# The forward 47-point stage of a Fourier mixing kernel, in four 64x64 quarters of TensorE's array

## The chip, the cores and the metric

One core of a Trainium2 chip runs the whole program. The metric is the device time of one execution in microseconds (us); the time before is the median of three runs.

## The reference

```python
X = np.fft.rfft(x, axis=1)                    # x: 8 batches, 3008 rows, 256 channels
y = np.fft.irfft(X * (filt_r + 1j * filt_i), n=3008, axis=1)
h = y.reshape(24064, 256) @ w_in              # 256 x 2048
s = np.sin(alpha * h)
return (h + s * s / (alpha + 1e-09)) @ w_out  # 2048 x 256
```

A filter is applied along the sequence in the frequency domain, and a two-layer network with a sine follows on each row.

## The kernel before, in words

**The transform.** 3008 is 47 x 64. A row of x is 64 m + r with m from 0 to 46 and r from 0 to 63, the residue. The forward transform is done in two stages: 47-point transforms over m for each residue (the stage that changes), then 64-point transforms over the residues for each of 24 kept frequencies. The spectrum is multiplied by the filter, and two inverse stages lead back. Data is fp16, sums are fp32.

**Batch 0** is kept on the chip (f1_chip, turn1, g_chip, turn2) and is not touched. **Batches 1 to 7** go by these steps, each a small function:

- load_x (L130 to L138) brings x to the tile xt by GpSimd's DMA queue, which turns fp32 into fp16. A partition holds one m and one of two residue groups (a = 0 for residues 0 to 31, a = 1 for 32 to 63), 94 partitions; along the partition lie the 32 residues of the group, 256 channels each. Each part of a load is two transfers (80 and 14 partitions). Batch 1 comes in four parts, the others in two.
- f1 (L140 to L152) is the 47-point stage. Its table wa is block-diagonal: 94 rows (two groups of 47) by 96 columns (two groups of 24 real and 24 imaginary parts), with zeros between the groups. Unit u, of 16, multiplies it with residues 2u and 2u + 1 of both groups (512 moving elements, L145) into one PSUM bank, psa. ScalarE copies even units to the tile asb, VectorE odd ones (L146). After units 7 and 15, SyncE stores half of asb to scratch memory (L150).
- shuffle1 (L197 to L202) reads the scratch back in another order as bint, in three transfers on SyncE's queue (the gather).
- f2x (L204 to L211) is the 64-point stage, product (L213 to L229) the filter, f2g (L231) the first inverse stage, with a scratch store and shuffle2 (L246) as gather; f3 (L252) is the second inverse stage, which writes yt, the network's input.

**The network.** For each chunk g of 512 rows (47 chunks) mlp_in (L276) makes 16 blocks of 128 hidden units: two matmuls of 512 moving elements into a bank ph (L281) and a sine on ScalarE (L283). VectorE squares them (L288), and the previous chunk's second layer goes by mlp_out (L300) or, for some chunks, by fast_out (L380), which uses seven block products instead of eight with sums on VectorE (L331, L391).

**What sets the order.** The program order is written by hand. The loop over g has eight slots a chunk; each slot has two mlp_in calls with parts of the previous chunk's second layer between them. A plan gives for each half slot the steps of the transform that are put there, so that batch b's transform runs inside the network of batch b - 1. For batches 2 to 7 two f1 units stand in the first half of each of eight slots; for batch 1 one unit stands in each of sixteen half slots, from slot 4 on. shuffle1 is put eight slots after the first unit, the first f2x at slot x0, and load_x of the next batch near the last product. Each engine works its instructions in order; each DMA queue does so too. GpSimd's queue carries the loads of x, the filter and the weights, in this order for batch 1: w_in (L602), x of batch 1, w_out (L452). SyncE's queue carries the scratch stores, the gathers and the output. PSUM banks for f1, f2x, f2g, f3 and parts of the set-up come from one pool, psf, of three. xt and bint share one buffer, so a batch's x is loaded once bint of the batch before is read.

At the start there is one small matmul for alpha (psal, L446: a 16-row fp32 operand), followed by matmuls on zeros that keep TensorE busy (keep_busy, L496).

Of the kernel before, what the change touches and what calls it, by code (L numbers as in the profile page):

```python
# [9 lines left out]
FP16 = mybir.dt.float16  # L10
FP32 = mybir.dt.float32
# [3 lines left out]
B, S, C, DFF = 8, 3008, 256, 2048  # L15
MT, R, NK, RP = 47, 64, 24, 32
GT = 2 * MT


def dft_tables():  # L20

    m = np.arange(MT)
    k1 = np.arange(NK)
    ang = 2 * np.pi * np.outer(m, k1) / MT
    fa = np.concatenate([np.cos(ang), -np.sin(ang)], 1) / np.sqrt(MT)
    wa = np.zeros((MT, 2, 2, 2 * NK))
    wa[:, 0, 0] = fa  # L30
    wa[:, 1, 1] = fa
    wa = wa.reshape(2 * MT, 4 * NK)
    wa2 = wa.reshape(2 * MT, 4, NK).transpose(0, 2, 1).reshape(2 * MT, 4 * NK)

    we = wa.T.copy()
    we2 = wa2.T.copy()
    r = np.arange(R)
    wb = np.zeros((2, R, NK, 128))
    wg = np.zeros((128, NK, 2, R))
    q = 1 / np.sqrt(R)  # L40
    d, j, di, ji = slice(0, 32), slice(32, 64), slice(64, 96), slice(96, 128)
    for s in range(NK):
        kd = s + MT * np.arange(32)
        kj = MT * np.arange(1, 33) - s
        td = 2 * np.pi * (np.outer(r, kd) % S) / S
        tj = 2 * np.pi * (np.outer(r, kj) % S) / S
        cd, sd, cj, sj = np.cos(td) * q, np.sin(td) * q, np.cos(tj) * q, np.sin(tj) * q
        wb[0, :, s, d], wb[1, :, s, d], wb[0, :, s, di], wb[1, :, s, di] = (
            cd, sd, -sd, cd)
        wb[0, :, s, j], wb[1, :, s, j], wb[0, :, s, ji], wb[1, :, s, ji] = (  # L50
            cj, -sj, -sj, -cj)
        wd = np.where((kd == 0) | (kd == S // 2), 1.0, 2.0)[:, None]
        wj = np.where(kj == S // 2, 1.0, 0.0 if s == 0 else 2.0)[:, None]
        wg[d, s, 0], wg[di, s, 0], wg[d, s, 1], wg[di, s, 1] = (
            wd * v.T for v in (cd, -sd, sd, cd))
        wg[j, s, 0], wg[ji, s, 0], wg[j, s, 1], wg[ji, s, 1] = (
            wj * v.T for v in (cj, -sj, -sj, -cj))

    wb = wb.reshape(2, 2, RP, NK * 128).transpose(2, 1, 0, 3).reshape(128, NK * 128)
    wg = wg.reshape(128, NK, 2, 2, RP).transpose(0, 1, 4, 3, 2).reshape(128, NK * 128)  # L60
    wgs = np.concatenate([wg[64:], -wg[:64]], 0)
    return [a.astype(np.float16) for a in (wa, wb, wg, we, wa2, we2, wgs)]

@with_exitstack
def kernel(
# [10 lines left out]
    nc = tc.nc  # L76
# [3 lines left out]
    def dram(ap, off, dims):  # L80
        return bass.AP(tensor=ap.tensor, offset=ap.offset + off, ap=dims)

    wa_np, wb_np, wg_np, we_np, wa2_np, we2_np, wgs_np = dft_tables()
    wa_d = nc.inline_tensor(wa_np, name="wa_tbl")
    wb_d = nc.inline_tensor(wb_np, name="wb_tbl")
    wg_d = nc.inline_tensor(wg_np, name="wg_tbl")
    we_d = nc.inline_tensor(we_np, name="we_tbl")
# [6 lines left out]
    cpool = ctx.enter_context(tc.tile_pool(name="consts", bufs=1))  # L94
    xbpool = ctx.enter_context(tc.tile_pool(name="xbp", bufs=1))
# [3 lines left out]
    agpool = ctx.enter_context(tc.tile_pool(name="agp", bufs=1))  # L99
    ginpool = ctx.enter_context(tc.tile_pool(name="ginp", bufs=2))  # L100
    ypool = ctx.enter_context(tc.tile_pool(name="yp", bufs=4))
    vpool = ctx.enter_context(tc.tile_pool(name="vp", bufs=2))
# [3 lines left out]
    psf = ctx.enter_context(tc.tile_pool(name="psf", bufs=3, space=PSUM))  # L106
    psh = ctx.enter_context(tc.tile_pool(name="psh", bufs=3, space=PSUM))
    pso = ctx.enter_context(tc.tile_pool(name="pso", bufs=1, space=PSUM))

    wa = cpool.tile([GT, 4 * NK], FP16, name="wa")  # L110
    we = cpool.tile([4 * NK, GT], FP16, name="we")
    wa2 = cpool.tile([GT, 4 * NK], FP16, name="wa2")
    we2 = cpool.tile([4 * NK, GT], FP16, name="we2")
    wb = cpool.tile([128, NK * 128], FP16, name="wb")
    wg = cpool.tile([128, NK * 128], FP16, name="wg")
# [6 lines left out]
    xt, asb, scr1, bint, xs, z, t2, gsb, scr2, gin, yt, vt, po, ot, x_dma, w_in_dma, filter_dma = (  # L122
        {} for _ in range(17))
# [5 lines left out]

    def load_x(b, parts=2):  # L130

        xt[b] = (xbpool if b else vpool).tile([GT, RP, C], FP16, name="xt", tag="xb" if b else "vt")
        n = RP // parts
        for h in range(parts):
            for p0, p1 in ((0, 80), (80, GT)):
                x_dma[b, h] = nc.gpsimd.dma_start(  # L136
                    out=xt[b][p0:p1, n * h:n * h + n, :],
                    in_=dram(x, (b * S + RP * p0 + n * h) * C, [[RP * C, p1 - p0], [1, n * C]]))  # L138

    def f1(b, u):  # L140
        if u == 0:
            asb[b] = agpool.tile([4 * NK, RP, C], FP16, name="asb", tag="ag")
            scr1[b] = dpool.tile([RP, 4 * NK, C], FP16, name="scr1", tag="scr1")
        ps = psf.tile([4 * NK, 2, C], FP32, name="psa", tag="f")
        nc.tensor.matmul(out=ps, lhsT=wa, rhs=xt[b][:, 2 * u:2 * u + 2, :], start=True, stop=True)  # L145
        (nc.vector.tensor_copy if u % 2 else nc.scalar.copy)(  # L146
            out=asb[b][:, 2 * u:2 * u + 2, :], in_=ps)
        if u % 8 == 7:
            k = 2 * u - 14
            nc.sync.dma_start(out=scr1[b][k:k + 16].rearrange("r q c -> q r c"),  # L150
                              in_=asb[b][:, k:k + 16, :])

    def f1_chip(k):

# [364 lines left out]
    def at(slot, f, *args):  # L519
        plan.setdefault(int(2 * slot), []).append((f, args))  # L520

    for b in range(1, B):
        p = MT * (b - 1)
        u0, x0, step = (4, 16, 1.1) if b == 1 else (p - 9, p + 4, 1.9)
        for u in range(16):
            at(u0 + u / 2 if b == 1 else u0 + u // 2, f1, b, u)
        at(u0 + 8, shuffle1, b)
        for k in range(6):
            xa, xb = x0 + int(2 * k * step), x0 + int((2 * k + 1) * step)
            at(xa, f2x, b, 2 * k)  # L530
            at(xb, f2x, b, 2 * k + 1)
            at(xb + 1, product, b, k, 0)
            at(xb + 2, product, b, k, 1)
            at(xb + 4, f2g, b, 2 * k)
            at(xb + 5, f2g, b, 2 * k + 1)
        at(xb + 6, shuffle2, b)
        if b + 1 < B:
            at(xb + 1, load_x, b + 1)
# [37 lines left out]
    with tc.manual_schedule():  # L576
# [2 lines left out]
        nc.scalar.dma_start(out=alpha_r, in_=moe_alpha.rearrange("(a p) -> a p", p=128))  # L579
        nc.scalar.dma_start(out=ident32, in_=id32_d.ap())  # L580
        nc.scalar.dma_start(out=we2, in_=we2_d.ap())
        nc.scalar.dma_start(out=wa, in_=wa_d.ap())
        nc.scalar.dma_start(out=we, in_=we_d.ap())
        nc.sync.dma_start(out=wb[:, 0:8 * 128], in_=wb_d.ap()[:, 0:8 * 128])
        zero = spool.tile([128, 512], FP16, name="zero", tag="z")
# [2 lines left out]
        nc.vector.memset(warm, 0.0)  # L588
        nc.scalar.activation(out=warm, in_=warm, func=AFT.Sin)
        load_x(0, 4)  # L590
        wgs = ginpool.tile([128, NK * 128], FP16, name="wgs", tag="gin")
        for s0 in (0, 8, 16):
# [6 lines left out]
        for h in range(2):  # L599
            hs = slice(1024 * h, 1024 * h + 1024)  # L600
            for cb in range(2):
                w_in_dma[h, cb] = nc.gpsimd.dma_start(out=w_in16[:, cb, hs],  # L602
                                                      in_=moe_w_in[128 * cb:128 * cb + 128, hs])
# [21 lines left out]
        for j in range(4):  # L625
            turn2(j)
        load_x(1, 4)
        load_w_out(0)
        load_w_out(1)
# [59 lines left out]
```

## Time and profile before

| what | value |
|---|---|
| median of 3 runs | 822.12 us (821.15 to 822.87) |
| the profiled execution | 823.99 us |
| its span, first to last instruction | 822.1 us |
| granted TensorE clock | 1.000 |
| L145 psa matmuls, 94x96 by 512 | 112, 381 ns each as recorded (median) |
| L145 weights loads of wa | 112, 124 ns |
| L146 copies to asb on ScalarE, VectorE | 56 of 584 ns, 56 of 682 ns |
| L136 loads of x on GpSimd's queue | 40 issues, 544 ns |
| L150 stores of asb on SyncE's queue | 14 issues, 324 ns |
| L201 gathers of bint on SyncE's queue | 21 issues, 424 ns |

A matmul's record is longer than the time for which it keeps the next one from starting, since matmuls are pipelined: how much of TensorE one takes is read from the start of one to the start of the next. PEld is the queue of weights loads, which runs beside the matmuls. Times in text are us from the span's start, if nothing else is said.

### The profile page before, as it was taken

What the parts mean: (1) busy time and instruction counts of PE and PEld (TensorE: products, weight loads), DVE (VectorE), ACT (ScalarE), POOL (GpSimd) and SP (SyncE); (2) the same over time, 40 slices, a digit from 0 to 9 for tenths busy, and PEclk for the clock granted to TensorE, in tenths of its full rate; (3) what the DMA queues carried; (4) which work ended last, traced back from release to release, by engine and by line L of the source; (5) the groups of instructions that cost most, each with busy time, mean ns of one, the idle gap of its engine ahead of it and who ended that gap; (6) DMA issues with size and microseconds to landing.
All of it is one profiled execution on the core that took longest, in us unless ns stands there. A gap on an engine that the chain in (4) does not pass through costs nothing.

```text
span 822.1 us, 17856 instructions
## 1 busy us (share of the span) xinstructions
PE 801.2 (97%) x7473; PEld 571.5 (70%) x7473; DVE 632.1 (77%) x856; ACT 630.1 (77%) x1179; POOL 39.6 (5%) x72
## 2 busy tenths in 40 slices
PE   6899999999999999999999999999999999999997
PEld 4557676777767776677667776677777677777776
DVE  4796986876769668686887778787889668888883
ACT  4796887787778877788777887778877787777773
POOL 6600010001000010000000010000100000000000
PEclk9999999999999999999999999999999999999999
DMA  9966375424543164612844147331564222411112
GB/s 195 187 109 242 104 185 115 143 70 117 139 117 116 52 171 94 196 50 61 186 102 144 52 97 184 94 113 53 127 155 114 93 71 91 98 44 36 28 53 52
DMA packets 67456, 91.44 MB, mean 111 GB/s; under 512 B 5512, under 2 KB 52376, under 8 KB 65864
## 3 DMA queue, kind: packets, MB, share of 16 engines
q1 hardware_dynamic: 58656, 68.90, 29.5%
q0 software_dynamic: 8192, 21.24, 12.8%
q8 instruction: 58, 0.95, 0.5%
q10 hardware_dynamic: 528, 0.18, 0.1%
q14 instruction: 22, 0.18, 0.1%
HBM read 59.62 MB, written 46.66 MB: 129 GB/s over the span
## 4 chain that ended last, share of the span: by engine, by line
PE 84%; DVE 5%; DMA 2%; issue 0%; ACT 0%; DVEq 0%
PE ph L281 35%; PE po L300 21%; PE pf L380 18%; PE psa L145 3%; PE psy L265 2%; PE psg L237 2%; PE psx L207 2%; DMA w_in<-in_moe_w_in_dram 1%; PE pe L411 1%; DVE vt L288 1%; DVE s L331 1%; DVE ot L422 1%; DVE t L227 1%; DMA bint<-scr 0%; DVE z L229 0%; DVE t L224 0%
## 5 line engine op out<-in xcount | busy, mean ns | idle before, releaser
L283 ACT ACTIVATE vt<-ph 128x512 f16<-128x512 f32 x688 | 408.5, 600 | 127.0 <-PE ph L281 120.0
L281 PE MATMUL ph<-yt,w_ina 128*128 128x512 f16 x1376 | 405.6, 379 | 0.0
L288 DVE TENSOR_TENSOR vt<-vt 128x2048 f16<-128x2048 f16 x188 | 229.5, 1221 | 75.1 <-ACT vt L283 73.7
L300 PE MATMUL po<-w_out,vt 128*128 128x256 f16 x1536 | 222.4, 272 | 1.7 <-DVE w_inT L470 1.0
L300 PEld LDWEIGHTS <-vt 128*128 128x128 f16 x1536 | 149.9, 98 | 91.5 <-issue 2.2
L281 PEld LDWEIGHTS <-w_ina 128*128 128x128 f16 x1376 | 117.2, 98 | 18.6
L380 PEld LDWEIGHTS <-s 128*128 128x128 f16 x1408 | 94.2, 98 | 41.7
L380 PEld LDWEIGHTS <-vt 128*128 128x128 f16 x1056 | 69.7, 98 | 37.2 <-DVE vt L288 7.1
L380 PE MATMUL pf<-tb,s 128*128 128x128 f16 x1056 | 84.0, 219 | 0.0
L391 DVE TENSOR_TENSOR ot<-pf,ot 128x512 f32<-128x512 f32 (+1 forms) x88 | 54.8, 622 | 32.2 <-PE pf L380 31.4
L211 ACT CAST xs<-psx 128x512 f16<-128x512 f32 x96 | 57.1, 605 | 6.8 <-PE psx L207 5.6
L239 ACT CAST gsb<-psg 128x512 f16<-128x512 f32 x84 | 49.4, 588 | 13.5 <-PE psg L237 11.9
L331 DVE TENSOR_TENSOR s<-vt 128x1024 f16<-128x1024 f16 (+1 forms) x66 | 57.0, 863 | 0.8
L380 PE MATMUL pf<-w_out,vt 128*128 128x128 f16 x704 | 53.8, 219 | 2.3 <-DVE ot L422 2.3
L146 DVE CAST asb<-psa 96x512 f16<-96x512 f32 x56 | 38.2, 682 | 18.7 <-PE psa L145 17.9
L283 ACT ACTIVATE vt<-ph,alpha_t 128x512 f16<-128x512 f32 x64 | 43.5, 700 | 9.9 <-PE ph L281 9.3
L267 ACT CAST yt<-psy 128x376 f16<-128x376 f32 (+45 forms) x126 | 45.7, 363 | 3.8 <-PE psy L265 0.3
L270 DVE CAST yt<-psy 128x240 f16<-128x240 f32 (+45 forms) x92 | 32.2, 349 | 20.3 <-ACT yt L267 19.1
L136 POOL DMA_DIRECT2D xt<-in_x_dram x40 | 21.5, 544 | 486.5 <-PE psy L265 298.4
L265 PE MATMUL psy<-we,gin 96*128 96x94 f16 x512 | 42.2, 204 | 0.0
L265 PEld LDWEIGHTS <-gin 96*128 96x128 f16 x512 | 34.2, 97 | 6.1 <-issue 0.4
L281 PE MATMUL ph<-yt,w_in 128*128 128x512 f16 x128 | 37.9, 379 | 0.0
(89 smaller groups left out, 747.1 us busy)
## 6 DMA issues: line engine op xcount, KB each, us to landing
scr<-asb SPq DMA_DIRECT2D x14, 768.0 KB
bint<-scr SPq DMA_DIRECT2D x21, 512.0 KB
scr<-gsb SPq DMA_DIRECT2D x21, 512.0 KB
out_dram<-ot SPq DMA_DIRECT2D x31, 320.0 KB
xt<-in_x_dram POOLq DMA_DIRECT2D x12, 640.0 KB, 7.9
gin<-scr SPq DMA_DIRECT2D x7, 768.0 KB
out_dram<-ot SPq DMA_DIRECT2D x16, 256.0 KB
gin<-scr SPq DMA_DIRECT2D x7, 576.0 KB
```

The lines of the kernel that those rows point to most:

```text
L146: (nc.vector.tensor_copy if u % 2 else nc.scalar.copy)(out=asb[b][:, 2 * u:2 * u + 2, :], in_=ps)
L211: nc.scalar.copy(out=xs[b, t // 2][:, t % 2 * 2:t % 2 * 2 + 2, :], in_=ps)
L239: nc.scalar.copy(out=gsb[b][:, 2 * t:2 * t + 2, :], in_=ps)
L265: nc.tensor.matmul(out=ps[:, t, :], lhsT=gin[b][:, 4 * a + t, 128 * cb:128 * cb + 128], rhs=we if b else we2, start=True, stop=True)
L267: (nc.vector.tensor_copy if G < 2 and cb == 0 else nc.scalar.copy)(out=yt[g][:, cb, :, lo:lo + n], in_=ps[:, :, 0:n])
L281: nc.tensor.matmul(out=ph, lhsT=(w_in16 if g < 4 else w_ina)[:, cb, 128 * jb:128 * jb + 128], rhs=yt[g][:, cb], start=(cb == 0), stop=(cb ...
L283: nc.scalar.activation(out=vt[g][:, jb, :], in_=ph, func=AFT.Sin, scale=alpha_t[:, jb:jb + 1] if g < 4 else 1.0)
L288: nc.vector.tensor_tensor(out=v4, in0=v4, in1=v4, op=ALU.mult)
L300: nc.tensor.matmul(out=po[g, h][:, i, :], lhsT=vt[g][:, k, ts] if k < 16 else yt[g][:, k - 16, t], rhs=w_out2[:, k, :] if k < 16 else m_t[ ...
L331: nc.vector.tensor_tensor(out=o, in0=a, in1=b, op=op)
L380: nc.tensor.matmul(out=ps[:, part, i], lhsT=a, rhs=b, start=first, stop=last)
L391: add = lambda out, in0, in1: nc.vector.tensor_tensor(out=out, in0=in0, in1=in1, op=ALU.add)
```

## The change

The block-diagonal table gives way to a table wq of 128 rows and 64 columns. Rows 0 to 46 and rows 64 to 110 hold the same 47-point table of 48 columns; the rest is zero. x of batches 1 to 7 lies on partitions 0 to 46 (residue group 0) and 64 to 110 (group 1), and each part is loaded by four transfers (32, 15, 32 and 15 partitions). A unit of f1 is now four residues of both groups, done by four matmuls with 47 rows and 64 columns: for each h (two residues each, in different column halves of the array and of the PSUM bank) and each a (residue group, in different row halves, into different banks). ScalarE copies the bank of group 0, VectorE that of group 1, 112 partitions each. There are 8 units a batch, and the store of half of asb is four transfers. The units of batches 2 to 7 stand in the same eight slots; those of batch 1 stand in slots 5 to 12, and its shuffle1 one slot later than before. Batch 0 and the inverse stages are left as they are.

```diff
+    wq = np.zeros((2, 64, 64))
+    wq[:, 0:MT, 0:2 * NK] = fa
+    wq = wq.reshape(128, 64)
...
-        xt[b] = (xbpool if b else vpool).tile([GT, RP, C], FP16, name="xt", tag="xb" if b else "vt")
+        xt[b] = (xbpool if b else vpool).tile([128 if b else GT, RP, C], FP16, name="xt", tag="xb" if b else "vt")
         n = RP // parts
         for h in range(parts):
-            for p0, p1 in ((0, 80), (80, GT)):
+            for p0, p1, row, step in (((0, 32, 0, R), (32, MT, 32 * R, R), (64, 96, RP, R), (96, 64 + MT, 32 * R + RP, R))
+                                      if b else ((0, 80, 0, RP), (80, GT, 80 * RP, RP))):
                 x_dma[b, h] = nc.gpsimd.dma_start(
                     out=xt[b][p0:p1, n * h:n * h + n, :],
-                    in_=dram(x, (b * S + RP * p0 + n * h) * C, [[RP * C, p1 - p0], [1, n * C]]))
+                    in_=dram(x, (b * S + row + n * h) * C, [[step * C, p1 - p0], [1, n * C]]))
...
-        ps = psf.tile([4 * NK, 2, C], FP32, name="psa", tag="f")
-        nc.tensor.matmul(out=ps, lhsT=wa, rhs=xt[b][:, 2 * u:2 * u + 2, :], start=True, stop=True)
-        (nc.vector.tensor_copy if u % 2 else nc.scalar.copy)(
-            out=asb[b][:, 2 * u:2 * u + 2, :], in_=ps)
-        if u % 8 == 7:
-            k = 2 * u - 14
-            nc.sync.dma_start(out=scr1[b][k:k + 16].rearrange("r q c -> q r c"),
-                              in_=asb[b][:, k:k + 16, :])
+        v, w = divmod(u, 4)
+        ps = [psf.tile([128, 2, C], FP32, name="psa", tag="f") for _ in range(2)]
+        for h in range(2):
+            r0 = 16 * v + 8 * h + 2 * w
+            for a in range(2):
+                nc.tensor.matmul(out=ps[a][64 * h:64 * h + 64], lhsT=wq[64 * a:64 * a + MT],
+                                 rhs=xt[b][64 * a:64 * a + MT, r0:r0 + 2, :], start=True, stop=True)
+        for a in range(2):
+            (nc.vector.tensor_copy if a else nc.scalar.copy)(
+                out=asb[b][0:112, a, 2 * u:2 * u + 2, :], in_=ps[a][0:112])
+        if w == 3:
+            for h in range(2):
+                r0 = 16 * v + 8 * h
+                for a in range(2):
+                    nc.sync.dma_start(
+                        out=scr1[b][r0:r0 + 8, 2 * NK * a:2 * NK * a + 2 * NK].rearrange("r q c -> q r c"),
+                        in_=asb[b][64 * h:64 * h + 2 * NK, a, 8 * v:8 * v + 8, :])
...
-        for u in range(16):
-            at(u0 + u / 2 if b == 1 else u0 + u // 2, f1, b, u)
-        at(u0 + 8, shuffle1, b)
+        for u in range(8):
+            at(u0 + u + (b == 1), f1, b, u)
+        at(u0 + 8 + (b == 1), shuffle1, b)
```

More of the change, by code (lines that the diff above doesn't have):

```diff
@@ L61, in dft_tables @@
     wgs = np.concatenate([wg[64:], -wg[:64]], 0)
-    return [a.astype(np.float16) for a in (wa, wb, wg, we, wa2, we2, wgs)]
+    return [a.astype(np.float16) for a in (wq, wb, wg, we, wa2, we2, wgs)]
 @with_exitstack
@@ L81, in dram @@
         return bass.AP(tensor=ap.tensor, offset=ap.offset + off, ap=dims)
-    wa_np, wb_np, wg_np, we_np, wa2_np, we2_np, wgs_np = dft_tables()
-    wa_d = nc.inline_tensor(wa_np, name="wa_tbl")
+    wq_np, wb_np, wg_np, we_np, wa2_np, we2_np, wgs_np = dft_tables()
+    wq_d = nc.inline_tensor(wq_np, name="wq_tbl")
     wb_d = nc.inline_tensor(wb_np, name="wb_tbl")
@@ L108 @@
     pso = ctx.enter_context(tc.tile_pool(name="pso", bufs=1, space=PSUM))
-    wa = cpool.tile([GT, 4 * NK], FP16, name="wa")
+    wq = cpool.tile([128, 64], FP16, name="wq")
     we = cpool.tile([4 * NK, GT], FP16, name="we")
@@ L136, in load_x @@
                 x_dma[b, h] = nc.gpsimd.dma_start(
                     out=xt[b][p0:p1, n * h:n * h + n, :],
-                    in_=dram(x, (b * S + RP * p0 + n * h) * C, [[RP * C, p1 - p0], [1, n * C]]))
+                    in_=dram(x, (b * S + row + n * h) * C, [[step * C, p1 - p0], [1, n * C]]))
     def f1(b, u):
         if u == 0:
-            asb[b] = agpool.tile([4 * NK, RP, C], FP16, name="asb", tag="ag")
+            asb[b] = agpool.tile([128, 2, RP // 2, C], FP16, name="asb", tag="ag")
@@ L581 @@
         nc.scalar.dma_start(out=we2, in_=we2_d.ap())
-        nc.scalar.dma_start(out=wa, in_=wa_d.ap())
+        nc.scalar.dma_start(out=wq, in_=wq_d.ap())
         nc.scalar.dma_start(out=we, in_=we_d.ap())
```

## The prediction, as put on record

> **What bounds the kernel now.** I read the page's busy shares first, then its chain of what ended last, then the stretches in which the changed stage runs, then single instructions there.
>
> ```profile
> PE 801.2 (97%) x7473; PEld 571.5 (70%) x7473; DVE 632.1 (77%) x856; ACT 630.1 (77%) x1179; POOL 39.6 (5%) x72
> ...
> PE 84%; DVE 5%; DMA 2%; issue 0%; ACT 0%; DVEq 0%
> PE ph L281 35%; PE po L300 21%; PE pf L380 18%; PE psa L145 3%; PE psy L265 2%; PE psg L237 2%; PE psx L207 2%; DMA w_in<-in_moe_w_in_dram 1%; PE pe L411 1%; DVE vt L288 1%; DVE s L331 1%; DVE ot L422 1%; DVE t L227 1%; DMA bint<-scr 0%; DVE z L229 0%; DVE t L224 0%
> ```
>
> The second line gives the chain to TensorE (84%), and in the third the stage that changes (psa, L145) holds 3% of the span, about 25 us. The stretches of batches 2 and 3, by engine:
>
> ```profile
> core 0: us, PE busy (x) PEld busy (x) DVE busy (x) ACT busy (x) POOL busy (x), PEclk, DMA share, GB/s
> 124.70:142.00 17.30, 17.30 (x123) 11.39 (x122) 11.48 (x17) 13.33 (x26) 0.00 (x0) 1.00 0.49 113
> 221.80:239.00 17.20, 17.20 (x144) 11.53 (x142) 12.17 (x17) 13.65 (x26) 0.00 (x0) 1.00 0.30 77
> ```
>
> TensorE is never free there at the full granted clock; VectorE and ScalarE have 5 and 4 us to spare of 17. So each ns that the stage gains or loses on TensorE is a ns of the kernel. One pair of steps, in order of time:
>
> ```profile
> 224.24 0.60 PE L145 MATMUL psa<-xt,wa 94*96 94x512 f16 x2
> 224.67 0.33 PE L265 MATMUL psy<-we,gin 96*128 96x94 f16 x4
> ```
>
> Two psa matmuls hold the array for 0.435 us (224.24 to 224.67), 0.2175 each, though the record of one is 0.381 long: the last 0.16 us overlap the next. 112 of them make 24.4 us, which agrees with the 3%.
>
> **Removed and added on TensorE.** Removed: 112 matmuls of 94x96, 56 pairs of 0.435 us. Added: 56 groups of four matmuls (47 rows, 64 columns, 512 moving elements), each with its own weights load; the order of instructions shows 224 loads and matmuls in the places of 112. A group costs one stream of 512, plus three start distances d, plus what it costs to go from the whole array to quarters and back, 2s.
>
> The stream: 0.216 us, from the pair.
>
> d: below, a matmul's record starts some 0.002 us after its weights load's; above, the densest row, eight matmuls of 96 columns in 0.50 us with a mean of 0.206 (L158, start 7.70), is 0.042 from start to start. I take 0.02, so 0.06 for three.
>
> s: the trace has one place where two such instructions of different extent meet, a 16-row matmul ahead of the first whole-array one:
>
> ```profile
> 3.16 0.58 PE L446 MATMUL psal<-ident,alpha_r 16*128 16x16 f32 x2 [3.16 <-DMA ident<-id_tbl]
> 3.67 1.46 PE L496 MATMUL idle<-zero,ident 128*128 128x512 f16 x3
> ```
>
> and on the queue of weights loads
>
> ```profile
> 3.67 0.13 PEld L496 LDWEIGHTS <-ident 128*128 128x128 f16 x2
> ```
>
> The two psal matmuls end at 3.74 (3.16 + 0.58); the second is 0.371 long by its tile's view, so it starts at 3.37. The next weights load has no wait recorded, and still it starts only at 3.67, 0.07 before that end. At 224.46, beside the second psa matmul, a load starts with the matmul ahead of it. So something holds the load until the array is nearly empty (the fp32 type could be it as well as the 16 rows, and the clock there is half: loads 0.43 apart). With the same hold after a matmul of 0.381, the next starts at 0.31 instead of 0.217: s = 0.09. On entry I add 0.03, since a load of the narrow kind takes longer (wa 0.124, others 0.098) and is then not hidden. Bounds: s = 0 if only the type held it; s = 0.26 if the load waits for the whole record (0.163) and is itself exposed (0.098). I take 0.12 + 0.09 = 0.21 for both switches, by the only row there is.
>
> Group: 0.216 + 0.06 + 0.21 = 0.486, against 0.435: +0.051, times 56 = **+2.9 us**.
>
> The Trainium skill speaks against this change: "TensorEngine Tiling (Array Packing)", Tiling Modes, says that changing the tiling mode drains the engine. It gives no price; read strictly (the 0.26 end) the sum would be +20 us, and with the psal row, +2.9.
>
> **Evictions.** Still one ScalarE and one VectorE copy per two rows, 56 each, now 112x512 for 96x512. Means are 0.584 and 0.682 us, and the neighbours show that partitions do not set them (ScalarE xs, 128x512: 0.605). ScalarE's copy starts up to 0.22 us later, since its bank is whole only after the third matmul. Hidden by the spare 4 and 5 us; the psf pool gives two of three banks as before. Nothing.
>
> **SP.** Each of 14 stores of asb becomes four, of the same bytes in the same 512-byte pieces: 42 more issues of 0.32 us, three more (1.0 us) ahead of each first spectrum gather and of the out stores queued behind. The gather's chain:
>
> ```profile
> 630.00 0.32 SPq L150 DMA_DIRECT2D scr<-asb  x1
> 634.92 1.29 SPq L201 DMA_DIRECT2D bint<-scr  x3
> ```
>
> and among TensorE's waits
>
> ```profile
> PE psx L207 <- DMA bint<-scr: 0.7, 1, 0.7
> ```
>
> That is batch 7: the gather waits 4.9 us for the store and then takes 3.92 (chain of waits), and TensorE waits 0.7 us for it at 638. The other gathers (69.19, 147.41, 244.21, 340.92, 438.99, 535.98) start 5.1 us or more before their first psx, so they have over 1 us to give. For batch 7 the delay is between 0 (the quarters transfer while the next is issued) and 1.0; I take 0.5.
>
> Batch 1's units move: sixteen single steps of half a slot become eight groups, the last at slot 12, not 11.5. On VectorE it then comes behind the square at 64.99 (1.23 long), so its copy ends near 66.9, not 64.36. The gather goes from 69.19 to 71.7, or 72.7 with the three issues, and lands at 75.6 to 76.6; first psx: 75.85. Between 0 and 0.8; I take 0.4. Cover: the 2.7 us between 73.1 (landing now) and 75.85.
>
> **POOL.** x loads of batches 1 to 7 double in number (32 to 64; 0.53 us each). For batches 2 to 7 these are 2.1 us more ahead of f1, which starts 20 us after the first issue (104.97, 124.75) with a landing time of 8.1: hidden. For batch 1 the two w_out loads stand behind eight more issues:
>
> ```profile
> 39.08 1.84 POOL L452 DMA_DIRECT2D w_out<-in_moe_w_out_dram x2 [1.22 <-DMA xt<-in_x_dram]
> ```
>
> and on VectorE, their first reader:
>
> ```profile
> 51.59 0.47 DVE L457 TENSOR_SCALAR w_out<-w_out,recip 128x256 f16<-128x256 f16 x2
> ```
>
> POOL waits here for earlier loads, eight back (the sixth x load waits for the second w_in, w_out for the first x). So w_out now waits for the ninth x load. If bytes pace it (a part of x per 1.7 us, same bytes), it lands some 1.5 us later than 47 and is hidden by the 4.5 us to 51.59. If each wait costs the whole 8 us of a landing, the ninth is issued at 37.9, w_out at 45.9, and it lands at 54.7: VectorE would stand 3 us at L457 with asb copies and the square behind it, and TensorE behind those. I take 0, and keep 3 for the range.
>
> **Sum.** 2.9 + 0.5 + 0.4 = +3.8 us. The profiled execution took 823.99 us (span 822.1 and 1.9 around it): 827.8. It lies 1.87 over the median of the runs, 822.12, so on the median's scale: **825.9**, s alone moving it between 811 and 843.
>
> **Rivals.**
>
> *B, the switch is cheap: faster.* If the hold at 3.67 came from fp32 and s is 0, a group costs 0.276, saves 0.159, times 56 is 8.9; less 0.9 is -8.0: **814.1** (d = 0.004: 0.228, -11.6 + 0.9: 811.4; d = 0.042: 817.8). It decides at 2s + 3d = 0.219. For it: the stage is on the chain with all its time and nothing else is full. Against: the held load. By the Trainium skill, "TensorE: Matmul & The Clock Gate", Part 3, packed tiles start about 4 ns apart, which is B's lower figure; no row of before shows it.
>
> *C, the quarters do not all run side by side.* Quarters with the same 47 rows (h = 0 and 1) stream from the same partitions. If the second pair waits for the first, a group costs 0.435 + 0.04 + 0.21 = 0.685: +14.0 + 0.9, **837**; all four in turn, 0.87 + 0.21: +36, **859**. The same part of that page says that a weights load overlaps a matmul in flight only when the row groups differ, which would give C; the trace of before disagrees for the whole array (the load at 224.46 beside the psa matmul of the same rows), so C stays small.
>
> *D, strict drain:* s = 0.26: 0.216 + 0.06 + 0.52 = 0.796, +20.2 + 0.9: **843**.
>
> **Chances.** Forecast 0.42, of which 0.06 within 0.2% (1.6 us, about what a measurement of this kernel can tell from no change) and 0.36 slower; B 0.42, of which 0.36 faster by more than that and 0.06 within (a partly cheap switch); C 0.11, D 0.05. Faster 0.36, same 0.12, slower 0.52. The range, 811 to 838, holds the forecast, nearly all of B and C's first form; outside are B's extreme, the serial form, D: about 0.15 to 0.2. The forecast's own range is 822.5 to 832, so the two signs stand nearly even and the price of a switch decides.
>
> **What would show it.** From the first psa matmul of a group to the next other matmul: 0.49 us by the forecast, 0.23 to 0.34 by B, 0.69 or more by C, 0.8 by D. Within a group the four starts are 0.02 apart, or in pairs 0.2 apart (C). A weights load that starts 0.3 us after the last psa matmul shows the hold. TensorE's wait for bint at batch 7 should be 0.7 to 1.7 us; one at 76 means batch 1. VectorE's first L457 instruction (51.59) waiting on a DMA, with TensorE idle near 53, shows the POOL queue. I am wrong above all if the load at 3.67 was held by its type.

## The result and the profile after

The changed kernel takes **826.46 us** (median of 5 runs, 824.64 to 828.00) against 822.12 for the kernel before (5 runs, 821.15 to 823.32): ratio 1.0053, 95% interval 1.0033 to 1.0073. The forecast was 825.9. Its profiled execution took 827.52 us, with a span of 825.7. The sum came out; three of its terms did not, as the next lines show.

On the page, the busy shares and the chain of what ended last:

```profile
PE 803.3 (97%) x7585; PEld 563.4 (68%) x7585; DVE 632.8 (77%) x856; ACT 628.4 (76%) x1179; POOL 55.8 (7%) x104
...
PE 82%; DVE 5%; DMA 3%; issue 0%; ACT 0%; SPq 0%; DVEq 0%
PE ph L295 35%; PE po L314 20%; PE pf L394 18%; PE psy L279 2%; PE psg L251 2%; PE psa L154 2%; PE psx L221 2%; DMA w_in<-in_moe_w_in_dram 1%; DMA bint<-scr 1%; PE pe L425 1%; DVE vt L302 1%; DVE s L345 1%; DVE ot L436 1%; DMA scr<-asb 1%; DVE t L241 1%
```

TensorE's share of the chain fell from 84 to 82%, and two transfers stand in it with 1% each that had none or almost none: the gather (bint from scratch) and now the stores before it (scratch from asb). One group, in order of time (start, duration, engine, line):

```profile
225.11 0.50 PE L394 MATMUL pf<-w_out,s 128*128 128x128 f16 x6
225.54 0.41 PE L154 MATMUL psa<-xt,wq 47*64 47x512 f16 x4
225.88 0.34 PE L279 MATMUL psy<-we,gin 96*128 96x94 f16 x4
```

All four quarters are over 0.41 us after the first began, though each record is 0.400 long: they run side by side. The four starts, from the records, are at 0, 3 to 4, 7 and 10 ns. The next matmul starts 0.343 us after the first psa matmul. The weights loads at the same place:

```profile
225.00 0.43 PEld L394 LDWEIGHTS <-s 128*128 128x128 f16 x7
225.54 0.11 PEld L154 LDWEIGHTS <-wq 47*64 47x64 f16 x4
225.88 0.20 PEld L279 LDWEIGHTS <-gin 96*128 96x128 f16 x4 [0.23 <-issue]
```

The load queue is free from 225.43, but the first wq load waits to 225.54, and the load of the next whole-array matmul starts only at 225.88 with that matmul: both switches hold the loads. By the records, the step from the matmul ahead to the group's first is 0.149 us where it was 0.055 (0.203 for 0.109, 0.309 for 0.215, by the kind of matmul ahead): 0.094 more at nearly every place. So a group costs 0.343 + 0.094 = **0.437 us, where the pair cost 0.435**. The second to fifth matmul behind the group lose a little more: counted to the fifth, a group takes 0.010 to 0.012 us more than the pair did.

The gather, among TensorE's waits (us in total, times, longest):

```profile
PE psx L221 <- DMA bint<-scr: 2.9, 4, 1.5
```

It was 0.7, once. And on SyncE's queue, batch 7 and, before it, batch 3:

```profile
240.34 3.40 SPq L163 DMA_DIRECT2D scr<-asb  x4
247.90 1.29 SPq L215 DMA_DIRECT2D bint<-scr  x3
...
632.39 3.30 SPq L163 DMA_DIRECT2D scr<-asb  x4
638.94 1.29 SPq L215 DMA_DIRECT2D bint<-scr  x3
```

```profile
239.29 0.33 SPq L150 DMA_DIRECT2D scr<-asb  x1
244.21 1.29 SPq L201 DMA_DIRECT2D bint<-scr  x3
```

The last fence is the kernel before, batch 3. From the first store of the last half to the gather it took 4.9 us there, 7.6 and 6.5 after the change. Measured from the last copy to asb, the gather leaves after 5.3, 6.8, 7.5, 6.3, 7.0, 6.5 and 6.1 us in batches 1 to 7; before, after 4.8 to 5.0 in all. What that does to TensorE, batch 3 and then batch 7:

```profile
252.09 0.38 PE L221 MATMUL psx<-bint,wb 128*128 128x256 f16 x2 [0.98 <-DMA bint<-scr]
...
642.66 0.38 PE L221 MATMUL psx<-bint,wb 128*128 128x256 f16 x2 [1.51 <-DMA bint<-scr]
```

Where the time came from, by the time at which each chunk's first hidden block starts, after minus before. The start-up (to chunk 0, 37.6 us) differs by -0.7 and is set aside here: over the profiled executions of this study it scatters from -2.8 to +2.5 us between kernels.

| stretch | after minus before, us | what stands there |
|---|---|---|
| chunk 0 to 4 | +1.31 | batch 1's groups, one of them split by a bank wait; its gather 0.2 later; in chunk 3 to 4, +0.82, psg waits for VectorE |
| chunk 6 to 7 | +0.44 | batch 2's gather |
| chunk 12 to 13 | +1.15 | batch 3's gather |
| chunk 35 to 36 | +0.83 | batch 7's gather |
| all other | +0.60 | 0.18 at batch 4's gather (chunk 18 to 19); 0.02 to 0.10 in the chunks with groups of batches 2 to 7, 0.55 in all; nothing in the rest, and -0.13 at the end |
| chunk 0 to the end | **+4.33** | |

### The profile page after: what moved, and what is told of

The parts are those of the page before. It is cut to its first block, busy times and chain, and to the rows that moved or that the text cites. A ratio compares the mean times of both kernels' runs of the same rounds, so it can differ in the third digit from the quotient of the medians.

```text
span 825.7 us, 18210 instructions
## 1 busy us (share of the span) xinstructions
PE 803.3 (97%) x7585; PEld 563.4 (68%) x7585; DVE 632.8 (77%) x856; ACT 628.4 (76%) x1179; POOL 55.8 (7%) x104
## 4 chain that ended last, share of the span: by engine, by line
PE 82%; DVE 5%; DMA 3%; issue 0%; ACT 0%; SPq 0%; DVEq 0%
PE ph L295 35%; PE po L314 20%; PE pf L394 18%; PE psy L279 2%; PE psg L251 2%; PE psa L154 2%; PE psx L221 2%; DMA w_in<-in_moe_w_in_dram 1%; DMA bint<-scr 1%; PE pe L425 1%; DVE vt L302 1%; DVE s L345 1%; DVE ot L436 1%; DMA scr<-asb 1%; DVE t L241 1%
## 5 line engine op out<-in xcount | busy, mean ns | idle before, releaser
L295 PEld LDWEIGHTS <-w_ina 128*128 128x128 f16 x1376 | 114.7, 98 | 19.0 <-issue 7.3
L140 POOL DMA_DIRECT2D xt<-in_x_dram x72 | 37.7, 532 | 479.2 <-PE psy L279 293.9
L157 DVE CAST asb<-psa 112x512 f16<-112x512 f32 x56 | 38.4, 686 | 17.4 <-PE psa L154 17.0
L157 ACT CAST asb<-psa 112x512 f16<-112x512 f32 x56 | 33.1, 591 | 11.2 <-PE psa L154 10.6
L221 PE MATMUL psx<-bint,wb 128*128 128x256 f16 x192 | 36.3, 272 | 3.3 <-DMA bint<-scr 2.9
```

Source lines behind the costliest of these rows:

```text
L157: (nc.vector.tensor_copy if a else nc.scalar.copy)(out=asb[b][0:112, a, 2 * u:2 * u + 2, :], in_=ps[a][0:112])
L221: nc.tensor.matmul(out=ps[:, i, :], lhsT=wb[:, 128 * (2 * t + i):128 * (2 * t + i) + 128], rhs=bint[b][:, 2 * t + i, :], start=True, stop= ...
L295: nc.tensor.matmul(out=ph, lhsT=(w_in16 if g < 4 else w_ina)[:, cb, 128 * jb:128 * jb + 128], rhs=yt[g][:, cb], start=(cb == 0), stop=(cb ...
```

## Experiments

Two theories. **Gather**: the array gains and loses next to nothing (0.437 for 0.435), and the loss is the later gathers. **Array**: the four starts look cheap, but the switch costs TensorE more than they show, about the forecast's 2.9 us. Times are medians with the ratio to the kernel before on the same chip and its interval; "store" is the time from the batch's last copy to asb to the end of its last store packet (before: 4.3 to 4.5). Code is abridged to the lines that matter.

**Two stores for four.** From the changed kernel.

```diff
-asb: [128, 2, RP // 2, C]        four stores of 48 x 8 rows
+asb: [128, RP // 2, 2, C]        two stores of 48 x 16 rows
```

> The kernel after with the half-batch store of asb in two transfers of 384 KB, not four of 192 KB. Gather theory (the quarters themselves cost what the pairs did, and the time is lost where the spectrum gather comes late because four stores take 3.2 us to issue): a store gets out about 1 us sooner, TensorE's wait for bint falls from 2.9 us to about 1, and the time from 826.5 to about 824.8. Switch theory (going to quarters and back costs 2.9 us in all): the wait may fall, but the time stays at 826.

831.87 us, 1.0117 (1.0095 to 1.0139). A miss: it became slower. Fewer issues did not make the store faster (6.1 to 6.5 us, gather at 6.6 to 7.2), and batch 1's gather left behind other loads. TensorE's waits between 70 and 100 us, in the run with two stores:

```profile
PE psx L220 <- DMA bint<-scr: 5.8, 1, 5.8
```

It left at 74.27, after POOL had issued the alpha and w_in loads (72.61 and 73.33). In the changed kernel it left at 70.72, between the two (70.49 and 71.22), and was waited for 0.2 us. Of the 3.5 us between the two times, 2.1 belong to the whole execution, whose chunk 0 began that much later: the gather was 1.4 us later against its neighbours, and that cost 5.6. From 74 to 83 us the DMA engines were 84% busy; that the loads ahead are the reason is read from this order and was not tried by itself. So the number of issues is not what makes the gather late, which my 0.3 us an issue had assumed.

**Groups two slots earlier.** Batches 2 to 7 of the changed kernel; nothing but the place in the plan.

```diff
-            at(u0 + u + (b == 1), f1, b, u)
-        at(u0 + 8 + (b == 1), shuffle1, b)
+            at(u0 + u + (1 if b == 1 else -2), f1, b, u)
+        at(u0 + 8 + (1 if b == 1 else -2), shuffle1, b)
```

> The kernel after with the forward stage and the gather of batches 2 to 7 two slots (about 4.5 us) earlier in the plan; all else the same. Gather theory: the waits for bint of batches 2, 3 and 7 are gone (2.6 of 2.9 us), the time falls to about 823.9, and what is left over before is batch 1. Switch theory: 826 or more, since every group still costs the same on TensorE.

823.59 us, 1.0016 (1.0000 to 1.0031): 2.9 us back. The gathers of batches 2 to 7 leave as late after the copies as in the changed kernel (5.9 to 7.1), but nobody waits for those of batches 2 to 7 (all that is left is one wait of batch 1):

```profile
PE psx L221 <- DMA bint<-scr: 0.7, 1, 0.7
```

From chunk 0 to the end its profile is 0.4 us shorter than that of the kernel before. 56 groups of quarters are in it. Gather theory holds, array theory falls. The 1.4 us by which its median still stands over the kernel before are not in that stretch; they stay unexplained.

**Four stores before the change**, and **all but the array**. Both from the kernel before; the second also has four transfers for a part of x and batch 1's units in slots 5 to 12 with the gather one slot later.

```diff
+for h in range(2):
+    for a in range(2):      # 48 partitions, 8 rows each
+        nc.sync.dma_start(out=scr1[b][r0:r0 + 8, 48 * a:48 * a + 48]..., in_=asb[b][48 * a:48 * a + 48, r0:r0 + 8, :])
```

> The kernel before, whole array, with each store of asb cut in four transfers of the shape that the change has (48 partitions by 8 residues). Gather theory: gathers 1 to 2.5 us later, TensorE waits for bint at batches 2, 3 and 7 some 2.9 us in all where it was 0.7, time 822.1 + 2.2 = 824.3. Switch theory: no wait worth naming, 822.1 to 822.6.

> The kernel before, whole array and block-diagonal table, with everything else of the change: four stores, four loads a part for batches 1 to 7, batch 1's units in pairs at slots 5 to 12 with its gather one slot later. Gather theory: the whole loss without the quarters, 825.5 to 826.5. Switch theory: 823.0 to 823.6, the 0.9 us that the prediction gave to these parts. If the loads or batch 1's plan are the cause, it stands over the kernel with four stores alone by 1 us or more, with the difference before 100 us.

822.71 us, 1.0002 (0.9987 to 1.0018), and 822.62, 1.0004 (0.9991 to 1.0016). No loss where the gather theory of both had one; the second lies below both of its ranges. But here two of the four stores leave before the last copies, as rows come free in another order; their gathers leave at 3.5 to 5.8. So this does not yet acquit the four stores.

**Stores late.** The kernel before with the units in the change's order of residues, so that all four stores come free together.

```diff
+        r = 16 * (u // 8) + 8 * (u % 2) + 2 * (u % 8 // 2)
-        nc.tensor.matmul(out=ps, lhsT=wa, rhs=xt[b][:, 2 * u:2 * u + 2, :], start=True, stop=True)
+        nc.tensor.matmul(out=ps, lhsT=wa, rhs=xt[b][:, r:r + 2, :], start=True, stop=True)
```

> The kernel before, whole array, with its units in the change's order of residues, so that the four stores of 48 partitions by 8 residues become free together after the last two units, as they do in the change (with the units in their old order, two of the four went out early). Gather theory: from the last copy to the gather's issue 6 to 7.4 us instead of 4.9, TensorE's waits for bint 2 to 3 us instead of 0.7, time 824 to 824.8. If that is not it and the quarters cost the time: 4.9 us, 0.7 us, 822.2.

822.62 us, 1.0000 (0.9984 to 1.0016). Batch 3 in this run:

```profile
240.54 2.40 SPq L154 DMA_DIRECT2D scr<-asb  x4
245.84 1.29 SPq L206 DMA_DIRECT2D bint<-scr  x3
```

Four stores, issued together, take 2.4 us to issue and not 3.4, and the gather leaves 5.3 us after the first (5.0 after the last copy; 4.9 to 5.4 in batches 2 to 7). So neither their number nor their coming together makes the 7 us.

**A gap in the partitions.** The same, with the second residue group's results on partitions 64 to 111, where the change puts half of its own, by a table of 112 columns.

```diff
+    wc = np.zeros((GT, 112))
+    wc[:, 0:2 * NK] = wa[:, 0:2 * NK]
+    wc[:, 64:64 + 2 * NK] = wa[:, 2 * NK:]
-in_=asb[b][2 * NK * a:2 * NK * a + 2 * NK, r0:r0 + 8, :]
+in_=asb[b][64 * a:64 * a + 2 * NK, r0:r0 + 8, :]
```

> The kernel before, whole array, one matmul a unit as it was, its table padded to 112 columns so that the second residue group comes out on partitions 64 to 111 and not 48 to 95; units in the change's order, so that four 48x8 stores come free together as in the run with late stores, only that two of the four now leave from partitions 64 to 111. No quarters, no other loads, batch 1's plan untouched. Theory 'partitions': stores from partitions 0 to 47 and 64 to 111 take longer (in every kernel so far that had them there, a batch's store packets summed to 54 to 59 us and the last ended 5.2 to 6.9 us after the last eviction; 47 to 51 us and 4.4 to 4.7 us in every one that had them on 0 to 95): here last packet at +5.5 to +6.9, gather issued at +6 to +7.4, TensorE waits 2 to 3 us for the gathered batch, 824 to 825 us. Rival 'the quarters' (something else in the changed kernels makes the stores late, such as the two column halves' evictions and matmuls): +4.4 to +4.9 as in the run with late stores, waits under 1 us, 822.1 to 822.8.

822.01 us, 1.0008 (0.9995 to 1.0022). Every kernel so far with slow stores had them on these partitions, and still:

```profile
240.57 2.60 SPq L157 DMA_DIRECT2D scr<-asb  x4
246.02 1.29 SPq L209 DMA_DIRECT2D bint<-scr  x3
```

Store 4.5 to 4.9 us. The theory of the partitions falls.

**Another address, another order.** The changed kernel, with asb at another byte in each batch, and batch 6's stores by turns from the two partition blocks.

```diff
+    shift = {1: 48, 2: 32, 3: 48, 4: 64, 5: 96, 7: 32}
-            asb[b] = agpool.tile([128, 2, RP // 2, C], FP16, name="asb", tag="ag")
+            room = agpool.tile([128, RP * C + 96], FP16, name="asb", tag="ag")
+            o = shift.get(b, 0)
+            asb[b] = room[:, o:o + RP * C].rearrange("p (a r c) -> p a r c", a=2, c=C)
...
+            for h, a in ((0, 0), (1, 0), (0, 1), (1, 1)) if b == 6 else ((0, 0), (0, 1), (1, 0), (1, 1)):
```

> The changed kernel, nothing else changed than where asb lies: its tile has 192 bytes more, and each batch takes it from another byte. Before the change asb began 352 bytes past a multiple of 512, and in the kernel with the gap in partitions 384; both store fast (last packet 4.4 to 4.9 us after the last eviction). In the changed kernel it begins at 288, since the table in front of it is 64 bytes narrower, in the column halves at 416 and in the early groups with two tables at 480: all slow (5.2 to 6.8 us). Here batches 1 to 5 and 7 begin at 384, 352, 384, 416, 480 and 352; batch 6 stays at 288, but its four stores go out with the two partition blocks by turns. Theory 'address': batches 2, 3 and 7 store in 4.4 to 5.0 us, batches 4 and 5 stay at 5.8 to 6.8, batch 6 at about 5.9; the waits of TensorE for the gathered batch fall from 2.9 us to under 1.2, 824 to 825 us. Rival 'order' (two stores in a row from the same 48 partitions): batch 6 alone becomes fast, below 5; the waits stay, 826 to 827. Rival 'neither': all as in the changed kernel (4.8, 5.9, 6.8, 5.8, 6.5, 5.9, 5.5 for batches 1 to 7), 826 to 827; then the cause of the late stores stays open.

825.67 us, 1.0042 (1.0028 to 1.0055). Stores in batches 1 to 7: 4.6, 5.6, 6.2, 5.7, 6.3, 5.8 and 5.4 us, within 0.6 of the changed kernel's whatever the address or order. "Neither" holds on the stores, though the time came out 0.3 us better than it said. The address does count for the packets: the times of a store's 1536 add up to 54 to 55 us in the changed kernel, 56 to 57 at 64 and 96 bytes further, 59.5 at 128 and 62.4 at 192; the end of the store does not follow that. Batch 3, at an address that had stored fast in the kernel with the gap:

```profile
242.56 3.27 SPq L166 DMA_DIRECT2D scr<-asb  x4
249.54 1.29 SPq L218 DMA_DIRECT2D bint<-scr  x3
```

**Column halves alone.** The kernel before with each psa matmul cut in two of 94 rows and 64 columns.

```diff
+        for a in range(2):
+            nc.tensor.matmul(out=ps[64 * a:64 * a + 64], lhsT=wa[:, 64 * a:64 * a + 64],
+                             rhs=xt[b][:, 2 * u:2 * u + 2, :], start=True, stop=True)
```

> The kernel before with each psa matmul (94 rows by 96 columns) cut in two of 94 rows by 64 columns, in the two column halves of the array, streaming the same residues; one copy per unit as before, two stores for one. If going from whole columns to halves holds the engine as the quarters do: a pair of units costs 2 x 0.216 + 0.01 + 0.21 = 0.65 instead of 0.435, batch 1's single ones 0.43, in all 48 x 0.215 + 16 x 0.21 = +13.7, 835.8. If only the split of the rows does it: 0.44 a pair, 822.4, and up to 2 more for the two stores.

841.97 us, 1.0226 (1.0201 to 1.0252). The pair of units in this run:

```profile
228.26 0.62 PE L149 MATMUL psa<-xt,wa 94*64 94x512 f16 x4
228.82 0.34 PE L272 MATMUL psy<-we,gin 96*128 96x94 f16 x4
```

0.555 from the first to the next matmul and 0.094 more on entry make 0.649, where 0.65 was expected. Two halves of the same rows start 3 ns apart. They bring no work side by side that the whole matmul had not, so here the switch stands bare: 0.649 - 0.435 = 0.214 for each of 48 pairs, and 0.434 - 0.2175 = 0.217 for each of batch 1's 16 single units, 13.7 us of the 19.8 lost. Later stores (6.0 to 6.9 us, waits for bint 2.2) are part of the rest, which was not followed to its end.

**Row halves alone.** 47 rows and 128 columns, two matmuls a unit into two banks; twice the copies.

> The change's layout of x with the rows of the array split and the columns whole: each unit two matmuls of 47 rows by 128 columns into two banks, side by side, 16 units a batch, twice as many copies as before (48 partitions each). One look, for the time of a pair of units on TensorE, not for the total. If a split of the rows holds the engine: 0.65 us a pair of units, first start 0.09 late, next start 0.1 late; if only a split of the columns does: 0.44.

```diff
+            nc.tensor.matmul(out=ps[a], lhsT=wa[64 * a:64 * a + MT],   # 47 x 128
+                             rhs=xt[b][64 * a:64 * a + MT, r0:r0 + 2, :], start=True, stop=True)
```

885.44 us (one run), of which 25.4 are waits for banks, so the total says nothing of the switch. Its starts do: 0.096 to 0.097 more on entry, two halves 3 ns apart, 0.321 to 0.323 from the first to the next matmul where no bank is waited for. So row halves alone are held at both ends too.

**Two groups for one switch.** The early groups, with eight matmuls back to back in batches 2 to 7 and a fourth bank from the pool psh.

```diff
+        for w in range(2 * (j % 2), 2 * (j % 2) + 2):
...
+                first = w % 2 == 0 and a == 0
+                ps[w, a] = (psh if first else psf).tile([128, 2, C], FP32, name="psa", tag="ph" if first else "f")
```

> The change with the stage two slots earlier (823.6), and in batches 2 to 7 two groups of four quarter matmuls back to back, four banks (one of them from psh), so that 24 ways to quarters and back take the place of 48. If the 0.21 us is the price of going and coming back: a double group costs 2 x 0.216 + 0.03 + 0.21 = 0.66 instead of 0.87, 24 x 0.21 = 5.1 us less, 818.5. If it belongs to each group: 0.87 and 823.6. Waits for banks could take some of it back, up to 0.5 us each, and would show before the step behind the double group.

822.17 us, 0.9991 (0.9975 to 1.0007): a miss in the total. The pair of groups itself was as forecast: 0.094 on entry and 0.559 to the next matmul, 0.653 for what took 0.874 singly (the second group starts 0.240 after the first). But in 4 of 24 places a bank was not free, which took 1.5 us in all (at most 0.59), and 2.45 us went between chunks 2 and 4, mostly in waits of psg for VectorE (2.3 us, batch 1).

**Batch 1 left as it was**, with single early groups in batches 2 to 7, and then with double ones.

```diff
+            if b == 1:
+                at(u0 + u / 2, f1_whole, b, u)     # the block-diagonal table, 16 units
```

> The changed kernel with batch 1 as it was before the change (block-diagonal table, two transfers a load, 16 units at half slots, its gather at slot 12), and batches 2 to 7 in quarters two slots earlier, as in the run with early groups (823.6). Theory: what was left of the loss there, 1.4 us, is batch 1's (its groups at slots 5 to 12 among evictions of VectorE that other work waits for), and the array nets 0.1 us a batch: 822.2 to 822.8, psg's wait for VectorE near 93 us gone. Rival 'the array nets more than the starts show, or the wider evictions cost': the loss stays, 823.3 to 823.8.

820.60 us, 0.9988 (0.9979 to 0.9996): under the range expected, and not for the reason given, since psg's wait for VectorE near 93 us, which was to be gone, is there. TensorE's waits before, after the change, and in this run:

```profile
PE psg L237 <- DVE yt L270: 0.4, 1, 0.4
PE psg L251 <- DVE yt L284: 1.5, 2, 1.2
PE psg L267 <- DVE yt L300: 1.2, 1, 1.2
```

With early groups and batch 1 in quarters it is not there at all. So the size of this wait does not go by batch 1's stage. From chunk 0 to the end the profile stands at +0.1 us against before, that of the early groups at -0.4, so batch 1's groups are not what lies between their medians. The profiles differ by 2.6 us in the start-up, where batch 0's inverse stage waits 3.1 us for VectorE's product (psg from z) in the early-groups run, 1.6 before, and under 0.2 here. Why it does not here is open; the runs of this kernel also scatter less (1.8 us, against 6.0).

> The same, with two groups back to back in batches 2 to 7, as in the run of double groups (822.2, where 2.45 us were lost between chunks 2 and 4 and 3.8 us won after chunk 4). Theory: with batch 1 as before, the loss near chunks 2 to 4 goes and the gain stays: 818.4 to 819.6, faster than before by 0.3 to 0.45%. Rival 'the loss near 90 us is of the plan as a whole, not of batch 1's quarters': 821 to 822.

**818.01 us, 0.9953 (0.9939 to 0.9968)**, the fastest of all, and 3.8 us below the kernel before on the same chip. From chunk 0 to the end its profile is 3.5 us shorter than before. One pair of groups that met a full bank, and the next, that did not:

```profile
220.82 0.99 PE L197 MATMUL psa<-xt,wq 47*64 47x512 f16 x8
221.75 0.60 PE L339 MATMUL ph<-yt,w_ina 128*128 128x512 f16 x2
...
225.53 0.63 PE L197 MATMUL psa<-xt,wq 47*64 47x512 f16 x8
226.09 0.61 PE L339 MATMUL ph<-yt,w_ina 128*128 128x512 f16 x2
```

24 pairs save 24 x (0.870 - 0.653) = 5.2 us; four wait for banks (0.37, 0.04, 0.60 and 0.49 us) and give 1.5 back: 3.7, against 3.5 measured.

## Why the prediction was right, and which steps were not

The forecast of +3.8 met +4.3, by terms that were off in opposite directions: +2.9 was 0.6, +0.5 was 2.4 and +0.4 was 1.3. That the total came out is luck.

- **Stream and switch: right in sum.** 0.216 and 2s = 0.21 were forecast. Measured: 0.094 on entry and 0.117 on exit (0.333 from the last quarter to the next matmul, less 0.216), 0.211. The mechanism, a weights load that is held, is what the runs show, and fp16 matmuls show it too, so it does not need fp32. That it fits to 0.001 is luck, since the only row for it stood at half the clock (loads 0.43 apart) and in fp32, and the two shares came out the other way round (0.12 and 0.09 forecast). Nor is it any change of extent: 94x96 matmuls stand next to 128x128 ones in the kernel before, and there a load starts beside the matmul ahead (224.46); what is held is the way to and from 47 rows or 64 columns. Rival B, which needed s = 0, is out, but its break-even was near: 2s + 3d is 0.221, and 0.219 decides. Out are C (starts 3 to 4 ns apart, the same rows too) and D as well.
- **The start distance d: the mis-sized term.** I took 0.02 between 0.002 and 0.042; it is 0.0033. The 0.06 for three is 0.010, so the group is 0.437 and not 0.486, and with what the matmuls behind it lose 0.011 over the pair: the +2.9 us is +0.6 (56 x 0.011). By the Trainium skill, "TensorE: Matmul & The Clock Gate", Part 3, packed tiles start about 4 ns apart: the trace agrees with that figure. It does not agree with its other rule, weights loads overlapping only where the row groups differ: halves of the same rows also start 3 ns apart.
- **A sign and a bound that were worked out wrongly.** From the first psa matmul of a group to the next other one, "0.49 us by the forecast" holds the 0.12 of entry, which comes ahead of the first; that stretch alone would be 0.37. It reads 0.343, which by the text's own list is nearer to B's 0.34, though the switch is there. And "s alone" moves the time down to 814; 811 needs a d of 0.004 too.
- **The gather: the step that failed.** That the others "have over 1 us to give" was read rightly (1.2 us at batch 2, 1.5 at batch 3); what failed is the delay held against it, no more than 1.0 by three issues. The gather leaves 1.1 to 2.5 us later in batches 2 to 7, since the stores themselves take longer and not only their issues; so batches 2 and 3 wait too, and batch 7 waits 0.8 us longer. +0.5 was 2.4 in the stretches of batches 2, 3 and 7. The early groups undo it, which shows that it is the loss.
- **Batch 1: +0.4 was +1.3** (chunks 0 to 4), by other waits than the one I named: bint 0.2 us, the group at 50.0 split by a full bank for 0.4, and 0.8 of psg held for VectorE in chunk 3 to 4. The last is not shown to come from batch 1's groups: it is as long with batch 1 left as it was, and absent with the groups in place.
- **POOL and evictions: right.** w_out is issued at 41.17, 2.1 us later than before, and VectorE reaches it without a wait:

```profile
50.67 0.26 DVE L284 CAST yt<-psy 128x104 f16<-128x104 f32 x1
50.84 0.87 DVE L471 TENSOR_SCALAR w_out<-w_out,recip 128x256 f16<-128x256 f16 x4
```

The copies of 112 partitions take 591 and 686 ns, for 584 and 682.

**What stays open**: why the changed kernel's stores (batches 2 to 7) take 5.5 to 6.8 us for the bytes that took 4.3 to 4.5. Shown not to be enough: four issues, coming free together, partitions 64 to 111, the address, the order. Little else is moved at that time: at most 33 KB in batches 2 to 6 and 0.18 MB in batch 7, beside the store's 0.79, and the kernel with the gap has the same 0.18 in batch 7 and stores in 4.6. The 1536 packets sum to 54 to 55 us, for 47 before and 50 to 51 with the gap, and the 16 landings of one store are spread over 1.4 to 3.3 us (batch 3), for 0.8 to 1.1 in the kernel with the gap. What the slow kernels share is a psa stage in halves or quarters, with the stores from its results; how that reaches a transfer was not found. The two kernels that leave batch 1 as it was show the same within one execution: batch 1 stores in 4.5 us, in one transfer, and batches 2 to 7 in 5.3 to 6.1, though batches 3, 5 and 7 use the same place for asb as batch 1 and, with two scratch buffers in turn, the same scratch. So neither place is enough to explain it. That the late gathers cost the time is shown; why they are late is not.

## What to carry to other kernels

Splitting the array pays by the switch: count the switches, not the matmuls, and put as much narrow work as the banks hold behind each (one group gained nothing here, two gained 0.22 us a pair). When a stage's output goes through memory, put the end of the store in the sum with bounds of its own, batch by batch, and look whether the consumer's slack holds the upper one. Where a total is met, compare its terms as well; here errors of opposite sign hid each other.

## What the runs showed of the hardware

- A change from the whole array to quarters, column halves or row halves held the first matmul and its weights load for 0.093 to 0.097 us, and the way back took 0.117 from a single group of quarters. Whole-array matmuls of 94x96 and 128x128 next to each other were not held.
- Quarters with the same 47 rows and different column halves run side by side, 3 to 4 ns apart; so do halves of either kind. A second group behind the first starts at 0.240 us and not at 0.216.
- The same bytes in the same 512-byte packets took 4.5 to 4.9 us in one kernel (the gap in the partitions) and 5.5 to 6.8 in another (the change), with little else on the queues. Their packets' times added up to 54 to 62 us by the address of the tile.
- One gather that left 1.4 us later against its neighbours took TensorE 5.6 us more, when two loads of 1 MB on another queue had been issued ahead of it (the run with two stores).
